# A decode layer on one core: the rest of w_mod and Wo loaded behind the first K chunks, and eight FFN weight slots in place of three

## The chip, the cores and the metric

The kernel runs on one core of one Trainium2 chip. The metric is device time in microseconds (us) of one execution. Engines are PE (matmul), PEld (its weight loads), DVE, ACT, POOL (GpSimd) and SP. SP, ACT and POOL also issue DMAs; "SPq" or "ACTq" in a profile is such an issue.

## The reference, cut to what matters

One token passes through one adaptive-layernorm layer: attention over a cache of 65,536 positions, then a gated FFN.

```python
mod = (silu(c) @ w_mod)                      # 6 x 1024 columns: sa, ca, ga, sb, cb, gb
h = layernorm(x) * (1 + ca) + sa
q = h @ wq                                   # 32 heads of 128
o = softmax(q k^T / sqrt(128)) v             # 4 KV heads, each 65536 x 128, 8 query heads each
x = x + ga * (o @ wo)
h = layernorm(x) * (1 + cb) + sb
x = x + gb * ((gelu(h @ w_gate) * (h @ w_up)) @ w_down)   # 1024 -> 3584 -> 1024
```

Everything is read once, in bf16: K and V are 134.2 MB, w_mod 12.6, wq 8.4, wo 8.4 and the FFN weights 22.0 MB. With a single token there is no reuse of a weight, so the work is a stream of bytes with small products behind it.

## The kernel before

K is processed in 32 chunks of 8192 rows (2.1 MB), 8 chunks to each KV head ("group"). PE transposes a chunk in 8 sub-blocks of 8 tiles, DVE (three of four sub-blocks) and ACT (the fourth) copy the result to SBUF, and PE forms the scores. After the eighth chunk of a group come the maximum and the exponentials; the products with V of a group run during the K chunks of the next one. K and V have three SBUF slots each.

The parts that the change touches. First the front: all of the w_mod matvec and the wo issues stand in the program before any K work.

```python
ev_modrest = matvec_cols(PD_MOD + 16, wm2_sb[:, :, :], NC_IN, 0, 32, mbf[:, B_SC:B_SC + 8],
                         waits=[("s_wm2", 32), ev_qT], inc_name="s_pe")
# ... wo_sb lies where wm2_sb lay
for i in range(nwo):
    emit("act", (lambda e, i=i: e.dma_start(wo_sb[:, i * hb:(i + 1) * hb, :], wo_r[:, i * hb:(i + 1) * hb, :])),
         waits=[ev_modrest], inc="s_wo", inc_by=16)
```

Then the loop over sub-blocks, the three FFN slots and the end of the attention:

```python
for e_sb in range(NE):
    emit_tr()
    pe_sc_subblock(e_sb)
    # ... at the end of a chunk:
    if q + 3 < NQ:
        issue_k(q + 3)
    evac_block(q)
    if kc == NK - 1:
        smalls_and_exp(g)
    # ... V products of group g - 1; Wo partial of group g - 2 at kc == 0

# FFN block n takes the slot of K chunk n - 3, or of FFN block n - 3
for n in range(min(3, len(ffn_items))):
    ffn_slot_use[n] = issue_ffn(n)
# last group:
for vc in range(NK):
    pe_pv_chunk(g, vc)
lsum_and_final(g)
pe_attn_partial(NG - 2)
pe_attn_partial(NG - 1)
```

The FFN weights come in 12 blocks of 1.835 MB: gate and up of 896 columns four times, then four blocks of w_down.

## Time and profile before

| | before |
|---|---|
| median of 16 runs, us | 490.89 (489.65 to 494.79) |
| bytes moved | 186.64 MB |
| PE busy | 314.1 us (64%) |
| two data queues, share of the 16 DMA engines | 48.1% + 45.3% |

The page of the kernel before; the two long rows cut the span into 40 slices of 12.2 us, DMA as busy share in tenths and the rate in GB/s:

```profile
span 489.7 us, 16425 instructions
DMA  8999999999985999999999999999999999419994
GB/s 329 419 421 424 423 430 407 387 425 414 402 335 185 364 417 427 426 419 419 415 389 412 422 426 424 430 371 423 426 403 399 419 427 426 206 40 386 383 386 162
```

Two dents stand out: one at slices 12 to 14 (185 GB/s) and one at slices 35 and 36 (40 GB/s). Between the first and the last slice the engines are full everywhere else. PE, at 64%, is not the limit.

Stretches of time of the kernel before. The columns are the stretch, its length, busy us of PE, PEld, DVE, ACT and POOL with the number of instructions, the granted PE clock, the DMA share and the rate in GB/s:

```profile
80.00:140.00 60.00, 47.74 (x1031) 45.78 (x1028) 37.54 (x57) 21.00 (x24) 0.00 (x0) 0.91 1.02 404
140.00:160.00 20.00, 14.77 (x278) 14.12 (x279) 10.38 (x19) 12.35 (x24) 0.00 (x0) 0.83 0.63 222
160.00:180.00 20.00, 16.62 (x442) 16.19 (x439) 11.99 (x18) 6.34 (x8) 0.00 (x0) 1.00 0.98 392
420.00:440.00 20.00, 12.11 (x408) 11.88 (x409) 4.13 (x26) 1.49 (x2) 0.00 (x0) 0.50 0.17 57
440.00:480.00 40.00, 12.24 (x418) 11.59 (x415) 3.64 (x24) 0.83 (x4) 0.00 (x0) 0.50 1.05 385
```

The chain of waits of the kernel before, in order of time (start us, us, what):

```profile
43.35 26.18 another core or an unknown queue
69.58 5.84 PE ps_dm L201 x213
75.42 2.23 issue
77.66 1.32 PE ps_dm L201 x43
79.41 0.61 ACTq L352
80.05 6.22 ACTq L352
86.30 5.31 ACTq L352
91.71 1.03 ACT ktT L404
...
139.57 0.61 ACT scbuf L437
...
153.83 0.61 ACT scbuf L437
...
412.83 12.68 DMA vslot<-in_A_v_cache_dram
425.56 1.88 PE ps_og L498 x64
427.86 3.42 PE ps_dm L534 x128
...
436.06 4.63 PE ps_og L685 x168
440.71 15.21 DMA kffn<-in_B_w_up_dram
```

The lines up to 153.83 explain the first dent. PE stands from 43.35 to 69.58 us; the list of waits names the cause that the chain could not: 46.2 us in two waits "PE ps_dm L201 <- DMA wm_sb<-in_w_mod_dram", the longer 26.2. Then comes the matvec (L201), then ACT spends 12.6 us on four DMA issues (L352), and only then does it copy its first transposed sub-block (L404). So the K chunks start late; the eighth one ends at 139.57 us. In windows of 2 us the engines have loaded everything that the slots can hold by about 145 us, and no slot comes free before the ninth chunk is done, at 153.83. The last lines explain the second dent: the last V product, two Wo partials (L534) and the layernorm run while only three FFN blocks are loaded and the fourth waits for the first FFN product (L685).

### The profile page before, as it was taken

How to read it: one execution, taken by the hardware profiler on the slowest of the kernel's cores; microseconds unless marked ns; L12 is line 12 of the kernel's file. 1: busy time of each engine (PE TensorE's matmuls, PEld its weight loads, DVE VectorE, ACT ScalarE, POOL GpSimd, SP SyncE). 2: the span in 40 equal slices, each digit the busy share in tenths (PEclk: the TensorE clock that was granted, in tenths of full speed). 3: DMA queues.
4: the chain of work that ended last, by engine and by line, in shares of the span. 5: the costliest groups of instructions: out<-in, count | busy, mean ns of one | idle time of the engine just before them, and what ended most of it. 6: DMA issues, size and time to landing. Idle time of an engine off the chain costs nothing.

```text
span 489.7 us, 16425 instructions
## 1 busy us (share of the span) xinstructions
PE 314.1 (64%) x7747; PEld 304.9 (62%) x7747; DVE 169.7 (35%) x333; ACT 115.4 (24%) x172; POOL 0.2 (0%) x4
## 2 busy tenths in 40 slices
PE   1053037498877979789988986988977433562242
PEld 1053037498867979779988985987977433462232
DVE  1100002187764745344645542554553000030001
ACT  0200000244465322253322225232233301010000
POOL 0000000000000000000000000000000000000000
PEclk9999999599988988676778775888796555555555
DMA  8999999999985999999999999999999999419994
GB/s 329 419 421 424 423 430 407 387 425 414 402 335 185 364 417 427 426 419 419 415 389 412 422 426 424 430 371 423 426 403 399 419 427 426 206 40 386 383 386 162
DMA packets 28610, 186.64 MB, mean 381 GB/s; under 512 B 1408, under 2 KB 9600, under 8 KB 18304
## 3 DMA queue, kind: packets, MB, share of 16 engines
q1 hardware_dynamic: 17632, 93.33, 48.1%
q10 hardware_dynamic: 10912, 92.28, 45.3%
q8 instruction: 60, 0.98, 0.8%
q14 instruction: 6, 0.05, 0.0%
HBM read 185.60 MB, written 0.00 MB: 379 GB/s over the span
## 4 chain that ended last, share of the span: by engine, by line
PE 51%; DMA 27%; issue 7%; another core or an unknown queue 5%; ACT 4%; DVE 3%; ACTq 3%; DVEq 0%
PE ps_tr L386 26%; DMA vslot<-in_A_v_cache_dram 12%; PE ps_sc L423 9%; PE ps_og L498 8%; DMA wq_sb<-in_A_wq_dram 6%; DMA kdn<-in_B_w_down_dram 5%; DMA kffn<-in_B_w_up_dram 3%; PE ps_dm L201 3%; ACTq L352 3%; ACT scbuf L437 1%; ACT pbuf L480 1%; PE ps_dm L534 1%; PE ps_og L685 1%; DVE ktT L400 1%
## 5 line engine op out<-in xcount | busy, mean ns | idle before, releaser
L386 PE MATMUL ps_tr<-ident_bf,kslot 128*128 128x128 bf16 x2048 | 189.3, 246 | 10.5 <-issue 10.5
L400 DVE COPY ktT<-ps_tr 128x1024 bf16<-128x1024 bf16 x192 | 129.9, 690 | 118.5 <-PE ps_tr L386 118.4
L386 PEld LDWEIGHTS ps_tr<-ident_bf,kslot 128*128 128x128 bf16 x2048 | 142.9, 110 | 11.8 <-issue 11.6
L404 ACT ACTIVATE ktT<-ps_tr 128x1024 bf16<-128x1024 bf16 x64 | 65.5, 1024 | 219.5 <-PE ps_tr L386 149.4
L423 PE MATMUL ps_sc<-misc_bf,ktT 128*128 128x8 bf16 x2048 | 93.6, 169 | 21.2 <-ACT ktT L404 11.5
L423 PEld LDWEIGHTS ps_sc<-misc_bf,ktT 128*128 128x128 bf16 x2048 | 85.5, 102 | 24.1 <-ACT ktT L404 12.0
L498 PE MATMUL ps_og<-pbuf,vslot 128*128 128x8 bf16 x2048 | 59.8, 175 | 36.3 <-DMA vslot<-in_A_v_cache_dram 31.5
L498 PEld LDWEIGHTS ps_og<-pbuf,vslot 128*128 128x128 bf16 x2048 | 56.9, 100 | 37.8 <-DMA vslot<-in_A_v_cache_dram 32.3
L201 PE MATMUL ps_dm<-misc_bf,wm_sb 128*128 128x1 bf16 x384 | 10.7, 165 | 48.4 <-DMA wm_sb<-in_w_mod_dram 46.2
L201 PEld LDWEIGHTS ps_dm<-misc_bf,wm_sb 128*128 128x128 bf16 x384 | 10.5, 104 | 48.7 <-DMA wm_sb<-in_w_mod_dram 46.4
L685 PE MATMUL ps_og<-misc_bf,kffn 128*128 128x1 bf16 x448 | 12.9, 165 | 21.1 <-DMA kffn<-in_B_w_up_dram 12.3
L685 PEld LDWEIGHTS ps_og<-misc_bf,kffn 128*128 128x128 bf16 x448 | 12.4, 104 | 21.6 <-DMA kffn<-in_B_w_up_dram 12.5
L480 ACT ACTIVATE pbuf<-scbuf,misc_f 128x512 bf16<-128x512 bf16 x32 | 22.6, 708 | 10.1 <-DVE misc_f L471 10.1
L437 ACT ACTIVATE scbuf<-ps_sc 128x512 bf16<-128x512 f32 x32 | 19.1, 597 | 23.3 <-PE ps_sc L423 23.3
L441 DVE TENSOR_REDUCE misc_f<-ps_sc 128x8 f32<-128x512 f32 x32 | 22.1, 692 | 6.4 <-ACT scbuf L437 2.7
L515 DVE RECIPROCAL misc_f<-ps_og 128x8 f32<-128x8 f32 x4 | 0.8, 209 | 63.1 <-PE ps_og L512 63.1
L705 PE MATMUL ps_dm<-misc_bf,kdn 128*128 128x1 bf16 x224 | 6.6, 165 | 12.1 <-DMA kdn<-in_B_w_down_dram 12.1
L705 PEld LDWEIGHTS ps_dm<-misc_bf,kdn 128*128 128x128 bf16 x224 | 6.3, 104 | 12.4 <-DMA kdn<-in_B_w_down_dram 12.4
L354 DVE COPY misc_f<-ps_dm 128x32 f32<-128x32 f32 x1 | 0.2, 193 | 35.4 <-PE ps_dm L201 35.4
L201 PE MATMUL ps_dm<-misc_bf,wq_sb 128*128 128x1 bf16 x256 | 7.1, 165 | 4.8 <-issue 2.8
L724 DVE COPY misc_f<-ps_og 128x7 f32<-128x7 f32 x4 | 0.7, 166 | 27.2 <-PE ps_og L685 27.2
L201 PEld LDWEIGHTS ps_dm<-misc_bf,wq_sb 128*128 128x128 bf16 x256 | 7.0, 104 | 4.9 <-issue 2.8
(94 smaller groups left out, 61.6 us busy)
## 6 DMA issues: line engine op xcount, KB each, us to landing
kslot<-in_A_k_cache_dram SPq DMA_DIRECT2D x32, 2048.0 KB, 12.5
vslot<-in_A_v_cache_dram ACTq DMA_DIRECT2D x32, 2048.0 KB, 14.0
wq_sb<-in_A_wq_dram ACTq DMA_DIRECT2D x2, 4096.0 KB, 25.9
wm_sb<-in_w_mod_dram ACTq DMA_DIRECT2D x2, 4096.0 KB, 60.3
wo_sb<-in_A_wo_dram ACTq DMA_DIRECT2D x4, 2048.0 KB, 20.5
kffn<-in_B_w_gate_dram SPq DMA_DIRECT2D x4, 1792.0 KB, 14.3
kffn<-in_B_w_up_dram SPq DMA_DIRECT2D x4, 1792.0 KB, 14.1
kdn<-in_B_w_down_dram SPq DMA_DIRECT2D x4, 1792.0 KB, 12.6
```

The source lines that it names most:

```text
L201: return e.matmul(ps_dm[:, out_col0 + cb:out_col0 + cb + 1], wbuf3[:, ci, (col_base + cb) * 128:(col_base + cb + 1) * 128], rhs_cols[:, ci ...
L352: emit("act", (lambda e, i=i: e.dma_start(wo_sb[:, i * hb:(i + 1) * hb, :], wo_r[:, i * hb:(i + 1) * hb, :])), waits=[ev_modrest], inc="s_ ...
L386: return e.matmul(ps_tr[:, bank, jj * 128:(jj + 1) * 128], kslots[slot][:, t, :], ident_bf[:, :], is_transpose=True)
L400: ev = emit("dve", lambda e, bank=bank, ks=ks: e.tensor_copy(ktT[:, ks, :, :].rearrange("p a d -> p (a d)"), ps_tr[:, bank, :]), waits=wai ...
L404: ev = emit("act", lambda e, bank=bank, ks=ks: e.activation(ktT[:, ks, :, :].rearrange("p a d -> p (a d)"), ps_tr[:, bank, :], ACTF.Copy), ...
L423: return e.matmul(ps_sc[:, bank, 8 * t:8 * t + 8], ktT[:, ks, jj, :], qT[:, 8 * g:8 * g + 8])
L437: ev = emit("act", lambda e, b=b, kc=kc, bank=bank: e.activation(scbuf[:, b, :, kc * T:(kc + 1) * T], ps_sc[:, bank, 0:T * 8].rearrange("p ...
L441: ev = emit("dve", lambda e, b=b, kc=kc, bank=bank: e.tensor_reduce(maxp[:, b * NK * 8 + kc * 8:b * NK * 8 + kc * 8 + 8], ps_sc[:, bank, 0 ...
L480: r = emit("act", lambda e, b=b, h=h: e.activation(pbuf[:, b, h, :], scbuf[:, b, h, :], ACTF.Exp, bias=mf[:, C_NB + 8 * b + h:C_NB + 8 * b ...
L498: return e.matmul(ps_og[:, b, PG_O:PG_O + 8], vslots[slot][:, t, :], pbuf[:, b, :, vc * T + t], start=(vc == 0 and t == 0), stop=(vc == NK ...
L685: return e.matmul(ps_og[:, bank, colb + cb:colb + cb + 1], kslots_ffn[slot][:, ci, cb * 128:(cb + 1) * 128], h2[:, ci:ci + 1], start=(ci = ...
L705: return e.matmul(ps_dm[:, PD_DN + kb * 8 + cb:PD_DN + kb * 8 + cb + 1], kslots_dn[slot][:, ki, cb * 128:(cb + 1) * 128], mbf[:, B_A + kb ...
```

## The change

The intent is to give the DMA engines work in both dents. The core of the diff:

```diff
+        xffn_offs = [O_WM2 + i * 16 * KiB for i in range(4)] + [O_WQ + 48 * KiB]
+        # five more FFN slots: four in wo's space, one in the score buffer
-        ev_modrest = matvec_cols(... waits=[("s_wm2", 32), ev_qT] ...)
-            emit("act", (lambda e, i=i: e.dma_start(wo_sb[...], wo_r[...])), waits=[ev_modrest], ...)
+        def emit_modrest_and_wo():
+            ev_modrest = matvec_cols(... same ...)
+                emit("gps", (lambda e, i=i: e.dma_start(wo_sb[...], wo_r[...])), waits=[ev_modrest], ...)
@@ loop over K chunks
             evac_block(q)
+            if q == min(2, NQ - 1):
+                emit_modrest_and_wo()
             if kc == NK - 1:
                 smalls_and_exp(g)
-                if kc == 0 and g >= 2:
-                    pe_attn_partial(g - 2)
                 if kc == NK - 1:
                     # ... rest of the V products
                     lsum_and_final(g - 1)
+                    pe_attn_partial(g - 1)
@@ FFN
+        # a slot in wo's space is free once its group's Wo partial is done; it also waits
+        # for the third-last V product: waits.append(("s_v", NQ - 2))
-            if n + 3 < len(ffn_items):
-                ffn_slot_use[n + 3] = issue_ffn(n + 3)
+            if n + NSLOT < len(ffn_items):            # NSLOT = 8
+                ffn_slot_use[n + NSLOT] = issue_ffn(n + NSLOT)
```

So there are three parts: the **front** (matvec and wo behind K chunk 2, wo issued from GpSimd), the **FFN slots**, and the **Wo partials** right behind their group.

## The prediction

In it, "modrest" is the matvec with the rest of w_mod, "wm2" the buffer of these weights, and K and V chunks are counted from 0, so that K 7 is the last one of group 0.

> **What bounds it now.** The DMA engines. The page gives 186.64 MB over a 489.7 us span; the two data queues take 48.1% + 45.3% of the 16 engines' time. By stretches of time the DMA share is about 1.0 (415 to 429 GB/s; about 385 for wo and FFN weights) nearly everywhere. PE is only 64% busy, often at half clock. So time is won only where the DMA idles. Fine stretches show four places: the start (2 us), 140–154 us (7.6 us idle), 421–440 us (16.7 us idle), and the tail after the last weight block landed at 484.6 us.
>
> **Why the holes exist.**
> - 140–154 us: in the chain of waits PE stands 26 us for the rest of w_mod (43.3 to 69.6), then does 9.4 us of its matvec before any K transpose; ACT sits at four wo issues until 91.7, and PE waits 8 us for its evacuation. Group 0 ends at 139.6. During the exponentials K 8–10 and V 0–2 fill every slot, so nothing can be issued until K 8 is consumed (153.8).
> - 421–440 us: V has streamed in; only three FFN blocks were prefetched; the fourth waits for the first FFN product (437.7), behind the last V product, two Wo partials (3.55 us) and the layernorm chain.
>
> **The change.** (1) modrest and wo move behind K chunk 2, wo's issues from ACT to GpSimd. K 0 should land near 43 us; PE does three K chunks (5.6 us each at full clock, 8.5 at half) before w_mod's rest lands near 73. From 83 us K, V 0–2 and wo share the engines three ways. (The Trainium skill, "DMA: Bandwidth & Descriptors", Queues, rings and completion order: engines round-robin between queue rows; the landing time of wm2 agrees with equal shares.) That slows K, but group 0 ends near 124 us and K 8 is consumed near 138, while wo and K 8–10 keep the DMA busy to about 143. Gain: 6 to 8 us. The skill's "SBUF — State Buffer" (two separate sides) warns that GpSimd-issued DMAs can starve behind vector copies in a 2-port mode; wo is first needed after 200 us, so slack hides that.
>
> (2) FFN prefetch of eight blocks. Blocks 3–5 start after the third-last V product (417.7 us): 5.5 MB at about 390 GB/s plus the V remaining last until about 436. Blocks 6 and 7 are issued after the last Wo partial (about 432); freed slots follow from 439. V 31 shares the engines, so attention ends about 2.5 us later, less 1.8 us for the Wo partial moved forward. Gain: about 16 us.
>
> (3) Wo partials right behind their group's normalization stall PE near 1 us three times, in DMA-bound stages: no cost.
>
> The gain is hole filling, 7 + 17, less 0 to 3 us of new gaps.
>
> **Time: 466 us, range 460 to 474.** Faster by over 2% (below 480.9): 0.95; within 2%: 0.04; slower: 0.01.
>
> **Right if:** the DMA share has no low slice between 20 and about 460 us; PE's first transposes start near 44; the wait on w_mod shrinks to a few us; group 0's exponentials start near 125; FFN products 0–5 run without a DMA wait; the last four still wait for weights; the tail is unchanged.
>
> **Wrong if:** the GpSimd-issued wo moves slowly or drags the other queues; K is starved so long in group 0 that the hole stays; V 31's delay opens another gap; or steady-state chunks (10 us for K + V) turn PE-bound at half clock, wasting the gained start.

## The result, and the profile after

| | before | after |
|---|---|---|
| median, us | 490.89 (16 runs) | 464.23 (8 runs, 463.84 to 464.38) |
| ratio | | 0.9451 (95% interval 0.9432 to 0.9470) |
| mean rate over the span | 381 GB/s | 404 GB/s |
| K chunk 7 of group 0 ends (start of its last copy) | 139.57 us | 124.76 us |
| last V product starts | 425.56 us | 413.76 us |

A ratio is the mean time of one kernel's fast runs over that of the other's fast runs of the same rounds, so it is not quite the ratio of the medians. The output was correct. The change is 26.7 us faster.

The page after (slices of 11.6 us):

```profile
span 462.0 us, 16425 instructions
DMA  8999999999999999999999999999999999999993
GB/s 328 417 421 426 424 426 426 426 403 419 417 398 421 419 414 409 423 427 416 416 384 404 423 426 425 427 423 404 426 408 396 403 422 427 424 399 382 382 386 115
```

Both dents are gone. The first and the last slice are all that is left of idle DMA time.

The same stretches of time after, the last three at the FFN stage and the tail:

```profile
80.00:140.00 60.00, 46.29 (x1034) 44.20 (x1035) 28.33 (x46) 22.52 (x35) 3.65 (x4) 0.76 1.01 413
140.00:160.00 20.00, 17.60 (x414) 17.33 (x413) 12.68 (x20) 6.58 (x9) 0.00 (x0) 0.89 1.02 422
160.00:180.00 20.00, 17.70 (x393) 17.45 (x390) 9.60 (x15) 5.44 (x7) 0.00 (x0) 0.74 1.00 410
412.00:420.00 8.00, 4.17 (x130) 4.00 (x130) 1.67 (x11) 0.00 (x0) 0.00 (x0) 0.50 1.05 379
420.00:440.00 20.00, 12.33 (x426) 12.05 (x426) 5.01 (x33) 2.11 (x5) 0.00 (x0) 0.50 1.06 383
452.00:462.00 10.00, 3.57 (x113) 3.22 (x113) 1.27 (x7) 0.00 (x0) 0.00 (x0) 0.50 0.21 77
```

From 140 to 160 us the engines now move 422 GB/s, not 222. Half of what bridges the exponentials of group 0 is wo: from 124 to 140 us its queue moved 3.24 MB and that of K 3.10. And the layernorm and the first FFN products, which ran over idle queues before, now run while weights come in at 379 to 383 GB/s.

The chain of waits after, and the issue of wo in the timeline (start, us, engine, line, operation, what released it):

```profile
70.95 0.62 PE ps_tr L393 x8
...
72.40 11.04 another core or an unknown queue
83.48 5.39 PE ps_dm L205 x196
88.87 1.87 issue
90.74 1.74 PE ps_dm L205 x60
```

```profile
92.79 3.65 POOL L359 DMA_DIRECT2D wo_sb<-in_A_wo_dram  x4 [92.34 <-PE ps_dm L205]
```

PE now works on K from 48.02 us, and waits for w_mod only 11.0 us, from 72.40 to 83.48. The four wo issues take GpSimd 3.65 us and hold nobody.

### The profile page after: what moved, and what is told of

The parts are those of the page before. It is cut to its first block, busy times and chain, and to the rows that moved or that the text cites. A ratio compares the mean times of both kernels' runs of the same rounds, so it can differ in the third digit from the quotient of the medians.

```text
span 462.0 us, 16425 instructions
## 1 busy us (share of the span) xinstructions
PE 312.7 (68%) x7747; PEld 302.5 (65%) x7747; DVE 169.3 (37%) x333; ACT 115.4 (25%) x172; POOL 3.8 (1%) x8
## 3 DMA queue, kind: packets, MB, share of 16 engines
q0 software_dynamic: 2112, 8.39, 4.7%
## 4 chain that ended last, share of the span: by engine, by line
PE 50%; DMA 33%; issue 8%; DVE 3%; ACT 3%; another core or an unknown queue 2%; ACTq 0%
PE ps_tr L393 26%; DMA vslot<-in_A_v_cache_dram 15%; PE ps_sc L430 9%; PE ps_og L505 8%; DMA wq_sb<-in_A_wq_dram 7%; DMA kslot<-in_A_k_cache_dram 6%; DMA xdn<-in_B_w_down_dram 4%; PE ps_og L741 2%; PE ps_dm L205 2%; ACT pbuf L487 1%; ACT scbuf L444 1%; PE ps_dm L543 1%; DVE ktT L407 1%; DVE misc_f L448 0%
## 5 line engine op out<-in xcount | busy, mean ns | idle before, releaser
L393 PE MATMUL ps_tr<-ident_bf,kslot 128*128 128x128 bf16 x2048 | 186.7, 244 | 18.3 <-issue 10.2
L393 PEld LDWEIGHTS ps_tr<-ident_bf,kslot 128*128 128x128 bf16 x2048 | 140.0, 109 | 20.5 <-issue 12.1
L741 PE MATMUL ps_og<-misc_bf,xffn 128*128 128x1 bf16 x280 | 8.1, 165 | 7.9 <-issue 7.9
L741 PEld LDWEIGHTS ps_og<-misc_bf,xffn 128*128 128x128 bf16 x280 | 7.8, 104 | 8.2 <-issue 8.2
L543 PE MATMUL ps_dm<-misc_bf,wo_sb 128*128 128x1 bf16 x256 | 7.8, 166 | 3.2 <-DVE misc_bf L526 2.0
L543 PEld LDWEIGHTS ps_dm<-misc_bf,wo_sb 128*128 128x128 bf16 x256 | 7.3, 104 | 3.7 <-DVE misc_bf L526 2.4
L762 PE MATMUL ps_dm<-misc_bf,kdn 128*128 128x1 bf16 x168 | 5.1, 165 | 5.5 <-DMA kdn<-in_B_w_down_dram 5.4
L762 PEld LDWEIGHTS ps_dm<-misc_bf,kdn 128*128 128x128 bf16 x168 | 4.8, 104 | 5.8 <-DMA kdn<-in_B_w_down_dram 5.6
```

The lines of the kernel that those rows point to most:

```text
L393: return e.matmul(ps_tr[:, bank, jj * 128:(jj + 1) * 128], kslots[slot][:, t, :], ident_bf[:, :], is_transpose=True)
L543: return e.matmul(ps_dm[:, PD_ATT + g * 8 + cb:PD_ATT + g * 8 + cb + 1], wo_sb[:, h, cb * 128:(cb + 1) * 128], oT[:, h:h + 1], start=(hi = ...
L741: return e.matmul(ps_og[:, bank, colb + cb:colb + cb + 1], gu[:, ci, cb * 128:(cb + 1) * 128], h2[:, ci:ci + 1], start=(ci == 0), stop=(ci ...
L762: return e.matmul(ps_dm[:, PD_DN + kb * 8 + cb:PD_DN + kb * 8 + cb + 1], dn[:, ki, cb * 128:(cb + 1) * 128], mbf[:, B_A + kb * 7 + ki:B_A ...
```

## The experiments

The theory: the DMA queues are the only limit, the two dents are separate, and each part of the change is worth the bytes that it lets flow in its dent. All outputs are right. Each batch was measured beside the kernel before on the same chip.

### 1. The two halves alone

Front only (the kernel before with the front part of the diff above; FFN slots and Wo partials as before):

> The kernel before with only the front of the change: the rest of the w_mod matvec and the wo loads behind K chunk 2, wo issued from GpSimd; FFN prefetch and Wo partials as before. Theory (idle DMA time is the only thing that can be won, and the two parts fill two separate holes): the idle stretch at the first exponentials (7.6 us) disappears, the one before the FFN (16.7 us) stays; time near 483 us, 6 to 9 us below before. Rival (the front only shifts work, the DMA-bound middle swallows it, and the FFN prefetch gives all 26 us): within 2 us of before.

The rest only (the kernel after, with `ev_modrest` and wo's ACT issues back ahead of the K loop):

> The change without its front: modrest and wo as before, eight FFN slots and the moved Wo partials. Theory: the idle stretch before the FFN disappears, the one at the first exponentials stays; near 473 us, 16 to 19 us below before, and together with the front-only kernel the two gains add up to the 26.7 us of the whole change within 2 us. Rival (FFN prefetch gives all): near 464.

| kernel | median, us | gain on 491.06 |
|---|---|---|
| front only | 479.17 (479.13 to 479.19) | 11.9 |
| FFN slots and Wo partials only | 475.69 (475.42 to 476.10) | 15.4 |
| sum | | 27.3 |

The whole change gains 26.7 us, so the halves add up within the noise (each ratio is known to about 0.002, 1 us), as two separate holes must. The second half, 15.4 us, falls just short of the 16 to 19 expected. The rival, in which the middle of the kernel swallows the front's gain, is dead. But the front gave 11.9 us where 6 to 9 were expected. The stretches of the front-only kernel show why:

```profile
80.00:140.00 60.00, 45.17 (x1020) 42.92 (x1021) 27.68 (x45) 22.17 (x34) 3.64 (x4) 0.79 1.01 413
140.00:160.00 20.00, 18.17 (x407) 17.65 (x405) 12.70 (x20) 6.91 (x8) 0.00 (x0) 0.84 1.02 422
160.00:180.00 20.00, 16.71 (x422) 16.52 (x421) 10.14 (x15) 5.84 (x7) 0.00 (x0) 0.91 1.00 417
```

Multiply rate by time. From 80 to 180 us this kernel moved 413 x 60 + 422 x 20 + 417 x 20 = 41.56 MB; the kernel before 404 x 60 + 222 x 20 + 392 x 20 = 36.52 MB. The 5.04 MB between them take 12.0 us at 420 GB/s, and 11.9 were measured. The forecast had added up the *idle share* of the engines (7.6 us). That is too small a measure of a hole: from 140 to 160 us the engines counted as 63% busy, but moved only 222/422 = 53% of the bytes, and before and after the hole the rate was below 420 too.

### 2. Which part of the front: PE's order, or who issues wo?

One word changed in the kernel before (PE's order untouched):

```diff
-            emit("act", (lambda e, i=i: e.dma_start(wo_sb[...
+            emit("gps", (lambda e, i=i: e.dma_start(wo_sb[...
```

> The kernel before with one word changed: wo is issued from GpSimd, so ACT is no longer held for 12.6 us; the w_mod matvec stays ahead of the K transposes. Theory (the order on PE matters most, the held ACT is only part): K is then fed at half rate while wo streams, group 0 ends 3 to 6 us earlier, not 15; 2 to 4 us faster than before. Rival (the front gains by freeing ACT, not by the new PE order): as fast as the front-only kernel, near 483.

And the reverse: the front-only kernel with wo issued from ACT again, `emit("act", ...)` inside `emit_modrest_and_wo`:

> The front-only kernel with wo issued from ACT again. Theory: ACT is held by the four wo issues around 92 to 104 us, PE stalls about 8 us for its transposed-K copies, group 0 ends near 133 instead of 125, so about half of the idle stretch comes back; 2 to 5 us slower than front only. Rival (GpSimd issue buys nothing[...]): equal to or faster than front only.

| kernel | median, us | gain on 491.06 | K chunk 7 ends | MB from 80 to 180 us |
|---|---|---|---|---|
| before | 491.06 | | 139.57 us | 36.52 |
| new order on PE, wo from ACT | 486.90 (486.52 to 487.62) | 4.2 | 135.97 us | 38.08 |
| old order on PE, wo from GpSimd | 482.08 (481.07 to 486.11) | 9.0 | 131.59 us | 39.68 |
| both (front only) | 479.17 | 11.9 | 126.06 us | 41.56 |

The MB are worked out as above. Here my weights were upside down. The one word was worth about 9 us in the median, where 2 to 4 were expected; the new PE order without it was worth 4 (the interval of its ratio, 0.9898 to 0.9940, excludes 1). Going back to ACT costs the front-only kernel 7.7 us, more than the 2 to 5 expected. The timelines of ACT and one line of PE's show it, first of the kernel with the new order and wo from ACT, then ACT's of front only:

```profile
92.88 13.16 ACTq L355 DMA_DIRECT2D wo_sb<-in_A_wo_dram  x4
106.14 1.02 ACT L407 ACTIVATE ktT<-ps_tr 128x1024 bf16<-128x1024 bf16 x1 [33.15 <-issue]
107.22 0.37 PE L426 MATMUL ps_sc<-misc_bf,ktT 128*128 128x8 bf16 x8 [10.30 <-ACT ktT L407]
```

```profile
95.23 1.02 ACT L407 ACTIVATE ktT<-ps_tr 128x1024 bf16<-128x1024 bf16 x1 [23.72 <-PE ps_tr L389]
```

With four issues of 2 MB each, on the queue on which V 0 to 2 had been issued before, ACT is held 13.16 us. (Of the four in the kernel before, the quickest took 0.39 us and the slowest 6.22; that the queue was full by then is inferred, not shown. Other issues behind a burst on their queue were long too: ACT's second of w_mod took 14.95 us in the kernel before, SP's third FFN block in a row 8.21 after.) PE depends on ACT's copy in every fourth sub-block and waits 10.30 us for it, so the K chunk behind it ends at 111.90 instead of 100.83 us. About 10 us of this are left when K 8 is consumed and the next slot comes free, at 150.25 instead of 140.43 us. The moment at which the dent begins is no later: the engines run dry at about 143 us here and 145 in the kernel before. So a late K lengthens the dent at its end. The earlier K chunk 7 ends, the more bytes are moved by 180 us, in all four rows. Worked out from the missing bytes at 420 GB/s, the three gains are 3.7, 7.5 and 12.0 us.

Issuing from GpSimd also changed something else: wo went in 2,112 packets, as the profile counts them, of about 4 KB instead of 4,160 of 2 KB. That this is the gain is unlikely: from 80 to 140 us, where wo streams, the two kernels moved 411 and 413 GB/s. Issuing wo from SP was not tried.

The converse, that K would be starved by wo, did not happen: in the one-word kernel chunks 3 to 7 ended 6.2 to 6.6 us apart, against mostly 6.3 in the kernel before and 5.6 at the quickest. The traces show why. The first two lines are the queues of K (q1) and of w_mod (q10) in the kernel after from 44 to 80 us, the last two those of K and of wo (q0) from 104 to 124 us, from the view of the DMA queues, with packets, MB and share of the 16 engines:

```profile
q1 hardware_dynamic: 679, 9.81, 64.3%
q10 hardware_dynamic: 672, 5.37, 35.9%
q1 hardware_dynamic: 447, 6.54, 78.3%
q0 software_dynamic: 445, 1.79, 22.2%
```

Two queues with work sent nearly the same number of packets, so the bytes were shared by the size of a packet: about 14 KB for K, 8 KB for w_mod, 4 KB for wo. Beside wo, K kept 78% of the engines. (For pieces of 2 KB and less from SP or ACT the numbers of packets were not equal: from 406 to 413 us the FFN weights sent 517 packets and V 133.)

One thing stays open: the four runs of the one-word kernel spread over 5 us (481.07, 481.68, 482.49, 486.11), and the verdict on it is "unclear" (interval 0.9789 to 0.9881). Its profiled run was the slowest one; that trace loses bytes again at 300 to 320 us (393 GB/s against 422 before). So its gain is known only to about 5 to 10 us.

### 3. How many FFN slots fill the second dent?

In the kernel after, one line was added before `NSLOT` is taken, with k = 3, 4 and 6:

```diff
+        ffn_slots = ffn_slots[:k]
         NSLOT = len(ffn_slots)
```

> The changed kernel with three FFN slots instead of eight (the front and the moved Wo partials stay). Theory (each further block is 1.835 MB that would else be loaded after the attention, about 4.8 us at 385 GB/s, until the idle stretch is full): the stretch before the FFN is back, near 477.5 us; 1.7 us faster than the front-only kernel, by the one Wo partial taken from the end of the attention. Rival (the moved Wo partials give nothing): 479.

> Four FFN slots: one block more loaded during the end of the attention. Theory: 4.8 us faster than three slots, near 472.7. Rival (the early block takes its bandwidth from the last V loads, so that half is given back): 2.4 us faster, near 475.

> Six FFN slots, that is three more blocks before the attention ends. Theory: the stretch of about 15 us is nearly filled by three blocks of 4.8 us; within 1.5 us of the whole change, 464 to 466. Rival (all eight are needed): 468 or more.

| slots | median, us | last V product starts |
|---|---|---|
| 3 | 478.08 (477.64 to 478.43) | 413.66 us |
| 4 | 474.70 (473.12 to 476.62) | 415.43 us |
| 6 | 465.14 (464.44 to 465.25) | 414.16 us |
| 8 (the change; other chips) | 464.23 | 413.76 us |

The rate row of the page, three slots and then six:

```profile
GB/s 329 417 420 431 416 424 430 425 408 418 413 405 415 419 426 422 422 392 430 388 385 424 429 423 424 424 428 410 394 399 400 425 424 429 205 83 384 382 387 158
```

```profile
GB/s 324 418 422 419 427 425 424 428 411 406 420 401 419 408 413 426 425 411 405 428 424 398 419 424 421 414 387 402 424 422 396 401 425 428 426 396 341 386 386 158
```

With three slots the dent (205, 83) is back; with six it is nearly full (341 at the lowest), and the last two slots bring about 1 us. The last step is inside the noise of a comparison across chips. Slots five and six bring 9.6 us, 4.8 each, which is 1.835 MB at 385 GB/s, though the spread of the four-slot runs is in it. The fourth slot brings only 3.4, between the 4.8 and the 2.4 that were expected. Part of the difference is that the early block shares the engines with the last V load: the last V product starts 5.54 us after the one before it, against 4.86 with three slots, 5.48 with six and 5.83 with eight. So sharing delays the attention by 0.6 to 1.0 us, 0.7 here. (The other 1.1 us by which the last V product is later in the four-slot trace were there before its early block was issued, at 406.97: the third-last product starts at 405.00 us, against 403.90.) While the dent is open, a later attention moves everything after it, so 4.8 - 0.7 = 4.1 us could be expected. The rest is open: the four-slot runs spread over 3.5 us. That the delay costs nothing with eight slots, because the engines never run dry, is argued and not measured.

Three slots also isolate the moved Wo partials: against the front-only kernel, which differs only in them, the ratios to before are 0.9752 and 0.9760, no difference beyond the intervals (about 0.0025 each, 1.2 us), where 1.7 us were expected. From the start of the last V product to the first FFN product the front-only trace takes 10.51 us (413.42 to 423.93), the three-slot one 9.40 (413.66 to 423.06). So the traces show 1.1 us. The partial of group 2 had been running in the time in which the last partial waits for its normalization; without it PE stands still there.

### 4. The FFN stage itself: is 385 GB/s a limit of the queue or of the layout?

K and V, which lie contiguous for each partition over a whole chunk (16 KB), come at about 425 GB/s, the FFN weights at 385. Gate and up blocks are read in row pieces of 896 columns, 1792 B; w_down in rows of 2 KB. Three kernels cut the same 12 blocks of the same size otherwise:

```diff
 # down: 7 neighbouring rows per partition, 14 KB pieces
-        dn_r = B_w_down.rearrange("(k p) j -> p k j", p=128)
+        dn_r = B_w_down.rearrange("(k p q) j -> k p q j", p=128, q=7)
 # so hidden unit p*7+k must land on partition p: gate/up columns in steps of 7
-                                        gu[:, ci, cb * 128:(cb + 1) * 128],
+                                        gu[:, ci, cb:cb + 127 * 7 + 1:7],
 # gate/up: 4 of the 8 row blocks x 1792 columns, 3584 B pieces
-  gate_r[:, :, idx * 896:(idx + 1) * 896]
+  gate_r[:, 4 * idx[1]:4 * idx[1] + 4, idx[0] * 1792:(idx[0] + 1) * 1792]
 # (two blocks then make 14 columns; the GELU runs on 14 columns, twice)
```

The combined kernel first:

> The changed kernel with FFN weight blocks cut so that each row piece is longer, same bytes and same number of blocks: gate and up as 4 x 1792 columns (3584 B pieces instead of 1792 B), down with 7 neighbouring rows per partition (14 KB instead of 2 KB; the gate and up columns are taken in steps of 7 to match). Theory (the FFN loads run at 385 GB/s, not 425, because of their short pieces): the rate in the FFN stage rises to 415 to 425 GB/s, 22 MB take about 4 to 5 us less, near 460 us. Rival (385 GB/s is what one queue alone gives, or what is left by the engines' imbalance): same rate, within 1 us of the change, or slower by the stepped weight loads.

It took 460.70 us (459.90 to 462.40), near the 460 expected. Then each part alone, the combined kernel again and the change itself, on one chip:

> The changed kernel with only the down blocks relaid: 7 neighbouring rows per partition, 14 KB pieces instead of 2 KB; gate and up columns in steps of 7. Theory (piece length sets the rate of one DMA stream): 7.3 MB of 22 MB at about 428 instead of 385 GB/s, 1.9 us faster than the change, near 462.3. Rival (the gain of the combined kernel comes from the wide gate and up blocks alone): no change, 464.

> The changed kernel with only the gate and up blocks relaid: 3584 B pieces instead of 1792 B, plain columns. Theory: 14.7 MB at about 406 instead of 382 GB/s, 2.0 to 2.3 us faster than the change, near 462. Rival (all of the gain is the down blocks'): 464. Together with the down-only kernel the gains should add up to that of the combined kernel, 3.5 to 4 us.

> The combined relaid kernel again, on the same chip as the change itself: 3.5 us faster than the change, about 0.75%, its range of times not overlapping that of the change.

> The change itself, as the yardstick of the three relaid kernels on the same chip: near 464.2 us, as before.

| kernel | median, us | ratio to before | gain on the change |
|---|---|---|---|
| the change | 464.12 (464.00 to 467.84) | 0.9476 | |
| down relaid | 462.67 (462.50 to 462.71) | 0.9431 | 1.5 |
| gate and up relaid | 461.98 (461.70 to 462.50) | 0.9418 | 2.1 |
| both | 460.44 (460.14 to 460.63) | 0.9385 | 3.7 |

The gains add up, and none of the three ranges reaches that of the change (whose six runs include one of 467.84; the other five lie within 0.31 us). Stretches of the down-only kernel: while gate and up stream, then while w_down streams:

```profile
420.00:436.00 16.00, 13.47 (x244) 13.42 (x245) 3.49 (x22) 1.70 (x3) 0.00 (x0) 0.50 1.06 385
436.00:448.00 12.00, 12.00 (x247) 12.00 (x247) 2.21 (x15) 0.42 (x2) 0.00 (x0) 0.50 1.02 429
```

And of the kernel with both:

```profile
420.00:432.00 12.00, 9.52 (x176) 9.46 (x177) 1.75 (x10) 1.49 (x2) 0.00 (x0) 0.50 1.03 402
432.00:446.00 14.00, 14.00 (x266) 14.00 (x266) 1.13 (x7) 0.21 (x1) 0.00 (x0) 0.50 1.02 427
```

One queue alone gives 427 to 429 GB/s with 14 KB pieces, 402 with 3584 B and 385 with 1792 B, so it is the piece length, not the single queue. (A down block covers the same 1.835 MB of neighbouring bytes in both layouts, so there only the cut into pieces changed; SP's queue sent 3,072 packets fewer, one for each piece saved.) The stepped columns are paid by PE: its weight loads in the gate and up products take 153 ns instead of 104 in the first kernel with both, and PE is busy all of the 14 us. That hides under the stream here. This kernel, 460.44 us against 464.12 on the same chip, beats both the kernel before and the change.

## Why the prediction was right or wrong

The time was right (466 predicted, 464.23 measured), and so was the mechanism: two holes, filled separately. That the sum came so close is partly luck, as errors in its terms cancelled. Point by point:

- **"The gain is hole filling, 7 + 17".** Right in kind; both terms were off, in opposite directions. The front gave 11.9 us, not 6 to 8: the hole was measured by idle share, not by bytes. The FFN part gave 15.4 us by itself (14.6 us between the ratios 0.9760 and 0.9463, the mean of the two measured for the change, times 490.9), not 16 to 17.
- **"Group 0 ends near 124 us".** 124.76, and K 8 was consumed at 139.67 ("near 138"). This was luck: two errors cancelled. "w_mod's rest lands near 73": PE got it at 83.48, so the wait was 11.0 us, not "a few". "That slows K": it did not much; chunks 4 to 7 ended 6.3 us apart. Both come from one term, equal shares of the queues in bytes. The traces of Experiment 2 show nearly equal numbers of packets instead, so that K, with the longer ones, took 64% of the engines beside w_mod and 78% beside wo. After 44 us, w_mod's queue moved 6.09 MB up to 83.4 us; at half of 424 GB/s these would have been in at 73. The landing of w_mod in the kernel before (69.58 us), said to agree with equal shares, was no test: there K ran dry after three chunks, and w_mod then had all the engines, so that any split ends at the same time. And while both had work, from 44 to 60 us, K's queue moved 4.21 MB and w_mod's 2.55 there too.
- **"PE's first transposes start near 44".** 48.02. K 0, issued at 35.02, took 13 us.
- **ACT's part.** The prediction named it (ACT "sits at four wo issues until 91.7, and PE waits 8 us") but gave it no term of its own. Experiment 2 shows that it carried more than half of the front: 7.7 us are lost by putting it back.
- **"V 31 shares the engines, so attention ends about 2.5 us later".** About 1.0 us with eight slots (the last V product starts 5.83 us after the one before it, against 4.86 with three slots), 0.7 with four. The split was not equal here either: from 406 to 413 us V's queue moved 1.80 MB and the FFN's 0.93.
- **"Less 1.8 us for the Wo partial moved forward".** 1.1 us in the traces, as the old place had hidden a wait. In its new place each of the four partials waits about 0.5 us (2.0 in all), not the "near 1 us" of part (3).
- **"FFN products 0–5 run without a DMA wait; the last four still wait for weights; the tail is unchanged".** No DMA wait is named in the first six; PE stands 2.1 and 2.9 us there under "issue", which the profile explains by nothing. Of the last four, the down products, the first starts without a wait at 443.51 us and three wait 2.6 to 2.8 us each; they start 4.2 to 4.7 us apart, the pace of the loads. From the last product's start to the end it is 5.08 us before (484.62 to 489.7) and 5.07 after (456.93 to 462.0).
- **"Wo is first needed after 200 us, so slack hides that"** (the Trainium skill, "SBUF — State Buffer", SBUF: two separate sides, on DMAs from GpSimd that starve behind DVE). The last of wo's four loads landed at most 71.2 us after its issue, that is by 167 us at the latest; it was first used at 212.4. That it took 3.65 us for the four issues and sent as many packets as K from 104 to 124 us shows no starving there; whether any took place at other times, no run here shows.

## What to carry to other kernels

In a kernel that streams, find the stretches in which the DMA engines move fewer bytes than they can, and measure each in missing bytes, not in idle share; its worth in time is those bytes over the full rate, and separate holes add up. Ask which instruction frees the next slot, and follow it back to the engine that holds it up: here an engine that both computes and issues large DMAs was held 13 us by the issues alone. When two queues load at once, look at the packets of each in the profile before you assume equal shares. When no hole is left, look at the length of the contiguous pieces.

## What the Trainium skill lacked or had wrong

- "DMA: Bandwidth & Descriptors", Issuing engines are not separate DMA queues: it says that issuing from several engines only saves the sequencer's time to initiate, "which is usually small relative to the DMA itself". Behind loads issued before on the same queue, four issues of 2 MB held ACT for 12.61 us (13.16 in experiment 2, where it cost 7.7 us of the kernel's time), against 3.65 us on GpSimd for the same loads. The page lacks that an issue can hold the issuing engine's compute for microseconds. Its table Issuing engine by pattern gives simple loads to Sync and only indirect ones to GpSimd; that GpSimd can be the better place for a plain load than a busy ACT is missing.
- The same page, Why small descriptors are slow (HBM only): about 3 cycles of overhead per packet, with 32 bytes per beat. An estimate from that for 1792 B pieces is 3 of 59 cycles, 5%, and the 32 bytes of metadata that it names for each operation would add about 2%. Measured: 385 GB/s at 1792 B, 402 at 3584 B and 427 to 429 at 14 KB, so 10% and 6% below the long pieces. The page also lacks that pieces of about 2 KB are worth lengthening; it was worth 3.7 us here.
- The same page, Queues, rings and completion order: round-robin between queue rows by packet. The traces agree, with packets as the profile counts them, where the pieces were 4 KB and longer (679 and 672 packets of two queues from 44 to 80 us, 447 and 445 from 104 to 124). The page lacks what follows for the bytes, that the queue with the longer pieces gets the larger share: 64% to 36% for K beside w_mod. Equal shares in bytes gave w_mod at 73 us where 83.5 was measured.
